# A second softmax in another layout: maxima from scores with tokens on partitions, spread and added by products

## The chip, the core and the metric

The kernel runs on one core of a Trainium2 chip. Its engines work side by side, each through its own list of instructions in order: TensorE (PE) multiplies matrices and writes to PSUM, VectorE (DVE) and ScalarE (ACT) read and write PSUM and SBUF, SyncE (SP) issues the transfers from and to HBM. The metric is the time of one execution on the device in microseconds (us).

## What is computed

Cut to what matters, the reference is:

```python
def sm_attn(qq, kk, vv):                      # 8 batches, 8 heads, 64 wide
    s = scale * np.matmul(qq, kk.transpose(0, 1, 3, 2))
    s = s - np.max(s, axis=-1, keepdims=True)
    a = np.exp(s)
    a = a / (np.sum(a, axis=-1, keepdims=True) + 1e-09)
    return np.matmul(a, vv)
p_packed = sm_attn(p, k, v)                   # 32 pack queries over 576 tokens
out = sm_attn(q, p_packed, p_packed)          # 576 queries over the 32 packed tokens
x = out, heads side by side                   # (4608, 512)
g = x @ w_gate; val = x @ w_val               # 512 -> 1536
result = (g * sigmoid(g) * val) @ w_out       # 1536 -> 512
```

The *second softmax* is the one inside the second call: for each query and head over 32 scores.

## The kernel before

The batches are worked on one after the other. The attention matrix `a` of the second call is never multiplied with `p_packed` on its own: `p_packed` is multiplied with the gate and value weights first (the words `M`, tiles `mh` and `ml`), and `a`, in the tile `a2f`, is then the moving operand of the matmuls `g` that give gate and value directly. `a2f` has the 32 packed tokens of 4 head pairs on its 128 partitions and 2 x 576 columns: for each parity of the head (`par`) the queries.

The weights lie in HBM as 64-bit floats. A chunk of 1 MB is loaded as pairs of 32-bit words and turned into float32 by five steps: two on ACT (lines 189 and 190), three on DVE (191 to 193). Until this is done for the first chunks the work on them can't begin, and each batch needs the results of the attention first. So the first batch has a prologue. Its order on all engines is written out by hand: first as code, then as a list of words, `PROGRAM`, each of which issues some instructions (`W2` is the next of the five steps of weight chunk 2, `V0` one of output weight chunk 0, `M:1.0` the products of the packed tokens with chunk 2, `Mh:1.0` ACT's copies of them out of PSUM, `g0` to `g23` the gate and value matmuls, `silu` and `h` what follows them on ACT and DVE, `out0` the first matmul with the output weights, `s1_...` the first softmax of the next batch, `load_...` transfers). A word's instructions go to their engines in this order.

The second softmax of the first batch, before: it is done in two halves of 288 queries. `s2_mm` multiplies queries and packed tokens, with the tokens on partitions (32 for each head pair). DVE transposes blocks of 32x32 (`s2_block`, line 498), so that the 32 scores of a query lie side by side in a row; takes their maximum and subtracts it (`s2_max`, lines 512 and 513); ACT takes the exponential (line 517); DVE adds, inverts and scales (`s2_sums`, `s2_scale`, lines 524 to 530) and transposes back (`back`, line 771) into `a2f`. ACT then makes a rounded copy (`two_high`, line 851).

PE has filler in the prologue: `warm_up(n)` multiplies the identity with itself n times (line 705), 18 times ahead of `g0` and 25 times behind it (`warm25`). A product of float32 operands is two records in the trace. The PSUM banks come from three pools: `acc` (4), `gv` (2) and `aux` (2).

Of the kernel before, what the change touches and what calls it, by code (L numbers as in the profile page):

```python
# [10 lines left out]
F32 = mybir.dt.float32  # L11
# [21 lines left out]
NA, NB = 256, 320  # L33
NT = B * S
# [6 lines left out]
    W2 g0 W1 two_max1 two_high0 W2 warm25 W1 two_exp1 W2 W2 silu0 V0 h0 W2 V0 W1 load_w3 load_v1 M:1.0 two_sums1  # L41
    Mh:1.0 M:0.1 V0 Mh:0.1 two_scale1 g1 V0 silu1 two_back1 s1_scores0 h1 g2 two_high1 s1_max0 W3 V0 load_w4
# [82 lines left out]
def tile_pack_attention_swiglu(ctx: ExitStack, tc: tile.TileContext, qT, kT, v, vq, pT, wgv, wout, out):  # L125
# [16 lines left out]
    nc.gpsimd.memset(minus_two, -2.0)  # L142

# [85 lines left out]
    def load_k(b):  # L229
# [3 lines left out]
        if b == 0:  # L233
            qs[b] = io_tile(0, [P, 2, NHP, HS], F32, "q_t")
# [465 lines left out]
    with tc.manual_schedule(engines={mybir.EngineType.PE}):  # L700
# [15 lines left out]
        with tc.manual_schedule(  # L716
# [313 lines left out]
```

## Time and profile before

| | us |
|---|---|
| timed runs: median (lowest to highest) of 3 | 744.02 (743.64 to 744.34) |
| profiled execution: span from the first to the last instruction | 742.9 |
| median less span | 1.1 |
| PE, DVE, ACT busy in the span | 732.6, 454.2, 372.2 |

The profile is of one execution on the same chip type, and its time is its span; what a timed run has beside it lies before the first and after the last instruction. A row of a timeline gives start, duration, engine, line of the kernel, operation, output and inputs, shapes and count; in brackets stands how long the engine was idle before it and what ended that. `PE` rows are matmuls, `PEld` rows weight loads. A duration includes the tail of an instruction, which the next one overlaps, so the distance of two starts is often the better price.

### The profile page before, as it was taken

The page shows a single profiled execution, that of the slowest core. Times are in us where ns is not written, and L with a number is a line of the kernel's source. Part 1 is how long each engine was busy: PE and PEld are TensorE (multiplying, and loading weights), DVE is VectorE, ACT ScalarE, POOL GpSimd, SP SyncE. Part 2 cuts the span into 40 slices and gives each one's busy share as a digit, 9 for nine tenths or more (in the row PEclk, how much of TensorE's full clock was granted, in tenths as well). Part 3 has the DMA queues.
Part 4 walks back from the last instruction along what each step waited for, and adds up shares of the span by engine and source line. Part 5 has one row for each costly group of instructions (what it writes and reads, how often), then busy time and mean ns, then how long its engine had stood idle before and what let it go on. Part 6 is the DMA issues. An engine that isn't in the chain of part 4 may idle for free.

```text
span 742.9 us, 14217 instructions
## 1 busy us (share of the span) xinstructions
PE 732.6 (99%) x5808; PEld 602.4 (81%) x5808; DVE 454.2 (61%) x1008; ACT 372.2 (50%) x666; POOL 2.0 (0%) x13
## 2 busy tenths in 40 slices
PE   7999999999999999999999999999999999999997
PEld 4855767888888888888888888888888888888886
DVE  4988879665755547663765637655574555644333
ACT  3777845744635446563462535653453534533331
POOL 0000000000000000000000000000000000000000
PEclk9999999999999999999999999999999999999999
DMA  9686582310112201301112021001001000010001
GB/s 348 256 306 248 196 326 73 119 52 21 65 57 84 72 1 65 124 4 71 66 43 97 3 71 64 34 29 71 1 2 69 6 1 1 1 57 2 0 1 72
DMA packets 20001, 59.10 MB, mean 80 GB/s; under 512 B 5984, under 2 KB 7008, under 8 KB 17376
## 3 DMA queue, kind: packets, MB, share of 16 engines
q1 hardware_dynamic: 19792, 58.12, 21.7%
q8 instruction: 46, 0.75, 0.4%
q14 instruction: 19, 0.16, 0.1%
q10 hardware_dynamic: 144, 0.07, 0.0%
HBM read 48.69 MB, written 9.49 MB: 78 GB/s over the span
## 4 chain that ended last, share of the span: by engine, by line
PE 96%; DVE 1%; ACT 0%; issue 0%; DVEq 0%
PE gv L617 36%; PE acc L636 33%; PE aux L259 7%; PE gv L802 6%; PE aux L636 5%; PE acc L843 4%; PE gv_aux L471 2%; PE gv_aux L259 1%; PE gv_aux L388 1%; PE acc L705 1%; PE warm_ps L705 1%; ACT mh L584 0%; PE aux L335 0%; DVE w L192 0%; DVE ml L558 0%
## 5 line engine op out<-in xcount | busy, mean ns | idle before, releaser
L624 ACT ACTIVATE sg<-gv 128x256 f32<-128x256 f32 (+1 forms) x168 | 69.3, 412 | 180.4 <-PE gv L617 168.2
L628 DVE TENSOR_TENSOR hf<-gv,sg 128x256 f32<-128x256 f32 x168 | 71.1, 423 | 130.0 <-PE gv L617 119.2
L617 PE MATMUL gv<-a2h,ml 128*128 128x256 f32 (+1 forms) x672 | 143.6, 295 | 1.2 <-DVE t L827 1.2
L617 PE MATMUL gv<-a2l,mh 128*128 128x256 f32 (+1 forms) x672 | 144.2, 296 | 0.0
L617 PE MATMUL gv<-a2h,mh 128*128 128x256 f32 (+1 forms) x672 | 144.1, 296 | 0.0
L636 PE MATMUL acc<-wo_h,hl 128*128 128x512 f32 x344 | 140.8, 409 | 0.0
L636 PE MATMUL acc<-wo_l,hh 128*128 128x512 f32 x344 | 135.7, 395 | 0.0
L636 PE MATMUL acc<-wo_h,hh 128*128 128x512 f32 x344 | 134.3, 390 | 0.0
L617 PEld LDWEIGHTS gv<-a2h,ml 128*128 128x128 f32 x672 | 117.0, 189 | 15.6 <-issue 1.4
L170 ACT CAST hh<-hf 128x256 fp32r<-128x256 f32 x168 | 67.7, 403 | 102.5 <-DVE hf L628 102.4
L617 PEld LDWEIGHTS gv<-a2h,mh 128*128 128x128 f32 x672 | 108.6, 190 | 0.0
L617 PEld LDWEIGHTS gv<-a2l,mh 128*128 128x128 f32 x672 | 108.3, 189 | 0.0
L598 DVE TENSOR_TENSOR hl<-hf,hh 128x256 fp32r<-128x256 f32 x168 | 70.1, 417 | 46.4 <-ACT hh L170 46.3
L636 PEld LDWEIGHTS acc<-wo_h,hl 128*128 128x128 f32 x344 | 64.7, 188 | 27.7 <-issue 18.6
L636 PEld LDWEIGHTS acc<-wo_h,hh 128*128 128x128 f32 x344 | 64.6, 188 | 15.0
L636 PEld LDWEIGHTS acc<-wo_l,hh 128*128 128x128 f32 x344 | 64.8, 188 | 7.9 <-issue 0.5
L558 DVE TENSOR_TENSOR ml<-aux,mh 128x512 fp32r<-128x512 f32 x92 | 59.0, 683 | 3.9 <-ACT mh L584 3.8
L259 PE MATMUL aux<-w,ppt 64*32 64x512 f32 (+1 forms) x784 | 52.4, 588 | 0.5 <-ACT mh L584 0.5
L584 ACT CAST mh<-aux 128x512 fp32r<-128x512 f32 x92 | 49.4, 589 | 6.5 <-PE aux L259 1.9
L624 ACT ACT_TABLE_LOAD x30 | 38.5, 1283 | 14.0 <-PE gv L617 10.1
L843 PE MATMUL acc<-wo_f,h 128*128 128x512 f32 x80 | 37.2, 595 | 0.0
L843 PEld LDWEIGHTS acc<-wo_f,h 128*128 128x128 f32 x80 | 14.3, 189 | 13.8 <-issue 13.2
(152 smaller groups left out, 769.3 us busy)
## 6 DMA issues: line engine op xcount, KB each, us to landing
st<-in_wgv SPq DMA_DIRECT2D x12, 1024.0 KB, 6.5
k_t<-in_kT SPq DMA_DIRECT2D x16, 576.0 KB, 4.9
q_t<-in_qT SPq DMA_DIRECT2D x16, 576.0 KB, 4.8
out<-ot SPq DMA_DIRECT2D x36, 256.0 KB, 2.1
v_t<-in_vq SPq DMA_DIRECT2D x6, 1280.0 KB, 5.9
st<-in_wout SPq DMA_DIRECT2D x6, 1024.0 KB, 5.4
v_t<-in_v SPq DMA_DIRECT2D x2, 1024.0 KB, 8.8
p_t<-in_pT SPq DMA_DIRECT2D x7, 64.0 KB, 1.9
```

Of the source, the lines that this page charges most:

```text
L170: e.copy(dst, src)
L259: nc.tensor.matmul(outs[par][32 * hp : 32 * hp + 32], lhs(r, hp), rhs(r, hp), start=True, stop=True)
L471: nc.tensor.matmul(p_p[D * par : D * par + D, NP * hp : NP * hp + NP], v_t[:, par, hp, k, :], a1[:, par, hp, k, :], start=(k == 0), stop=( ...
L558: pin(nc.vector.tensor_tensor(*lows.pop(0), op=ALU.subtract))
L584: nc.scalar.copy(m[0][at], src)
L598: low = lo.tensor_tensor(hl, src, hh.bitcast(F32), op=ALU.subtract)
L617: nc.tensor.matmul(pg[:, :n], m_[:, g, f, s * P : (s + 1) * P], a_[:, g, off : off + n], start=(i == 0), stop=(i == 5),)
L624: nc.scalar.activation(sg[:, :n], pgs[0][:, :n], AF.Silu)
L628: nc.vector.tensor_tensor(hf, pgs[1][:, o : o + 256], sg[:, o : o + 256], op=ALU.mult)
L636: nc.tensor.matmul(acc[:, :], h_[:, c : c + P], w_[fc // 2][:, fc % 2], start=(fc == 0 and i == 0), stop=(fc == NFC - 1 and i == 2),)
L802: nc.tensor.matmul(held[i][s][:, :n], m_[:, g, f, s * P : (s + 1) * P], a_[:, g, off : off + n], start=(j == 0), stop=(j == len(todo) - 1),)
L843: nc.tensor.matmul(accs[2 * is_b + c], half(i)[:, c * P : c * P + P], wos[fc // 2][:, fc % 2], start=(fc == 0), stop=(fc == NFC - 1),)
```

## The change

For the first 256 of the 576 queries of the first batch the second softmax is done in another layout; the other 320 keep the old steps, in one piece. The parts are `PART[0]` and `PART[1]`, the same split that the `g` matmuls use.

- `z_tok` computes the scores of the 256 queries a second time with queries on partitions (128 at a time), so that the 32 scores of a head lie in a row; `z_max` takes their negative maxima from PSUM.
- `z_mm(0)` computes the scores with tokens on partitions and leaves the PSUM sum open; `z_sub` adds to it the maxima, spread over the 32 tokens of each head by a product with the identity. `z_exp` is ACT's exponential out of PSUM into SBUF.
- `z_sum` adds the exponentials by a product with `head_of` (a 128x4 matrix of ones in each head's rows, made at the start by one DVE reduction); `z_inv` inverts; `z_bcast` spreads the inverses by products; `z_mul` multiplies into `a2f`. There is no transpose.
- The scale of the packed heads (`s1_scale`, DVE) becomes `one_scale`, two activations on ACT.
- Queries of the first batch lie in HBM in the order of the two parts and are loaded by two transfers of 512 and 640 KB.
- The prologue from there on is written in words. Both fillers behind the pack are gone. `M:0.1` stands ahead of `g1` and `M:1.0` behind it.

```diff
 PROGRAM = """
-    W2 g0 W1 two_max1 two_high0 W2 warm25 W1 two_exp1 W2 W2 silu0 V0 h0 W2 V0 W1 load_w3 load_v1 M:1.0 two_sums1
-    Mh:1.0 M:0.1 V0 Mh:0.1 two_scale1 g1 V0 silu1 two_back1 s1_scores0 h1 g2 two_high1 s1_max0 W3 V0 load_w4
+    W0 W0 W0 W0 one_scale W0 one_flip one_ppt z_tok z_mm two_mm1 z_max z_sub0 z_sub1 M:0.0 z_exp0 z_exp1 load_k1
+    load_wout0 two_block1 z_sum z_inv z_bcast Mh:0.0 two_max1 W1 z_mul accs g0 W1 two_high0 W2 W1 W2 W1 W2 W1 two_exp1
+    silu0 W2 two_sums1 M:0.1 h0 W2 V0 Mh:0.1 load_w3 load_v1 g1 M:1.0 two_scale1 V0 Mh:1.0 silu1 V0 two_back1
+    h1 V0 s1_scores0 g2 two_high1 s1_max0 W3 V0 load_w4
...
+    def z_tok():
+        q_t, ppt = z_q(0), ppts[0]
+        pss = zs["tok"] = [gv_ps(), gv_ps()]
+        for t in range(NA // P):
+            for hp in range(NHP):
+                for par in range(NPAR):
+                    r = slice(64 * par, 64 * par + 64)
+                    at = t * P + NP * hp
+                    nc.tensor.matmul(
+                        pss[par][:, at : at + NP], q_t[r, hp, t * P : (t + 1) * P], ppt[r, NP * hp : NP * hp + NP],
+                        start=True, stop=True,
+                    )
...
+    def z_spread(at, row, par, add):
+        for t in range(NA // P):
+            for hp in range(NHP):
+                x = t * NHP + hp
+                nc.tensor.matmul(
+                    at[NP * hp : NP * hp + NP, t * P : (t + 1) * P],
+                    zs["m"][:, row, par, x : x + 1].broadcast_to([P, NP]), ident,
+                    start=not add, stop=not add or t == NA // P - 1,
+                )
...
+    def z_exp(par):
+        nc.scalar.activation(st2[0][0][:, par, :NA], zs["mm", 0][par][:, :NA], AF.Exp, scale=SCALE)
+    def z_sum():
...
+                    x[:, at : at + NHP], st2[0][0][:, par, t * P : (t + 1) * P], head_of, start=True, stop=True,
...
-            s1_scale(0)
...
-            m_mm(0, 0, c0, True)
-            m_high(0, 0, c0)
-            s2_max(0, c0)
-            s2_exp(0, c0)
-            s2_mm(0, 1)
-            s2_block(0, 1)
-            load_k(1)
-            load_wout(0)
-            warm_up(18)
...
-            s2_sums(0, c0)
-            s2_scale(0, c0)
-            back(0)
+            def one_scale():
+                pp = pool.tile([P, NPAR, D], F32, tag="pp", bufs=1, name="pp")
+                for par in range(NPAR):
+                    nc.scalar.activation(
+                        pp[:, par], pps[0][0][:, par * D : (par + 1) * D], AF.Copy,
+                        scale=st1[0][2][:, 2, par : par + 1],
+                    )
+            def z_mul():
+                nc.vector.tensor_tensor(
+                    z_head["a2f"][:, :, PART[0]], st2[0][0][:, :, PART[0]],
+                    zs["inv"].rearrange("p (r n) -> p r n", r=NPAR), op=ALU.mult,
+                )
```

What stands in each engine's list now, at three places. First PE, from the last score products of the softmax to the first ones of the next batch (`s1_scores0`, the row with `k_t`). In the program before, `L705` is filler, `L802` are `g0` and `g1`, and `L259` with `w_82` and `w_81` are `M:1.0` and `M:0.1`:

```order
L705 MATMUL warm_ps<-ident 128x128 x18
L802 MATMUL gv<-a2f,mh 128x256 x4
L705 MATMUL acc<-ident 128x128 x25
L259 MATMUL aux<-w_82,ppt 32x256 x8
L259 MATMUL aux<-w_81,ppt 32x256 x8
L802 MATMUL gv<-a2f,mh 128x256 x4
L259 MATMUL aux<-k_t,p_t 32x288 x8
```

In the changed program the lines have moved (`L268` is the old 259, `L924` the old 802); `L569` is `z_tok`, `L588` are `z_sub` and `z_bcast`, `L606` is `z_sum`, and `w_83` and `w_84` are the old `w_81` and `w_82`:

```order
L569 MATMUL gv_aux<-ppt,q_t 128x32 x16
L268 MATMUL acc_aux<-q_t,ppt 32x256 x8
L268 MATMUL acc_aux<-q_t,ppt 32x320 x8
L588 MATMUL acc_aux<-ident,zm 32x128 x16
L268 MATMUL aux<-w_83,ppt 32x256 x8
L606 MATMUL acc_aux<-head_of,s_244 128x4 x4
L588 MATMUL acc_aux<-ident,zm 32x128 x16
L924 MATMUL gv<-a2f,mh 128x256 x4
L268 MATMUL aux<-w_83,ppt 32x256 x8
L924 MATMUL gv<-a2f,mh 128x256 x4
L268 MATMUL aux<-w_84,ppt 32x256 x8
L268 MATMUL aux<-k_t,p_t 32x288 x8
```

Both fillers are gone, three kinds of small products have come in, and the first `w_83` products behind `g0` are followed by `g1` and only then by those of `w_84`.

Second ACT, from the rounded copy of the first attention part (`a2h`) to the silu of `g1`. Before:

```order
L851 CAST a2h<-a2f 128x2x288
L190 ACTIVATE st<-st,minus_two 128x1024
L517 ACTIVATE s_229<-s_229 128x576
L818 ACT_TABLE_LOAD
L818 ACTIVATE sg<-gv 128x256
L189 ACTIVATE wo_f<-st 128x1024
L190 ACTIVATE st<-st,minus_two 128x1024
L584 COPY mh<-aux 128x256 x4
L818 ACTIVATE sg<-gv 128x256
```

After (`L973` is the old 851, `L194` and `L195` the old 189 and 190, `L638` the exponential of the 320 queries, `L940` silu, `L702` the copies out of PSUM):

```order
L973 CAST a2h<-a2f 128x2x256
L194 ACTIVATE w_84<-st 128x4x256
L195 ACTIVATE st<-st,minus_two 128x1024
L638 ACTIVATE s_244<-s_244 128x2x320
L940 ACT_TABLE_LOAD
L940 ACTIVATE sg<-gv 128x256
L194 ACTIVATE wo_f<-st 128x1024
L702 COPY mh<-aux 128x256 x2
L195 ACTIVATE st<-st,minus_two 128x1024
L702 COPY mh<-aux 128x256 x2
L940 ACTIVATE sg<-gv 128x256
```

The two conversion steps of `w_84` now both stand behind the copy of `a2f`, and the second pair of copies is divided from the first by a conversion step of the output weights.

Third DVE, where the first attention part is finished. Before, from the sums of the first half (line 524) on:

```order
L524 TENSOR_REDUCE r_230<-s_229 128x18
L525 TENSOR_SCALAR r_230<-r_230 128x18
L526 RECIPROCAL r_230<-r_230 128x18
L530 TENSOR_TENSOR s_229<-s_229,r_230 128x576
L771 STREAM_TRANSPOSE a2f<-s_229 128x288 x2
L191 TENSOR_SCALAR w_81<-w_81 128x4x256
L512 TENSOR_REDUCE r_230<-s_229 128x18
L513 TENSOR_TENSOR s_229<-s_229,r_230 128x576
L192 SCALAR_TENSOR_TENSOR w_81<-w_81,st 128x4x256
```

After, from the maxima (`L578`) on; `L629` transposes the 320 queries, `L612` and `L613` are `z_inv`, `L633` and `L634` maximum and subtraction of the 320 queries, `L884` is `z_mul`:

```order
L578 TENSOR_REDUCE zm<-gv_aux 128x8 x2
L629 STREAM_TRANSPOSE s_244<-acc_aux 128x320 x2
L612 TENSOR_SCALAR zm<-acc_aux 128x16
L613 RECIPROCAL zm<-zm 128x16
L633 TENSOR_REDUCE r_245<-s_244 128x20
L634 TENSOR_TENSOR s_244<-s_244,r_245 128x2x320
L884 TENSOR_TENSOR a2f<-s_244,acc_aux 128x2x256
L196 TENSOR_SCALAR w_83<-w_83 128x4x256
L197 SCALAR_TENSOR_TENSOR w_83<-w_83,st 128x4x256
```

Sum, scale and back transposes of the first part are gone from DVE's list; the maximum and subtraction of the second part now stand ahead of the end of the first.

## Rows read from the trace of the kernel before

**Rows 1.** The page: span, and busy time of the engines in it.

```profile
span 742.9 us, 14217 instructions
...
PE 732.6 (99%) x5808; PEld 602.4 (81%) x5808; DVE 454.2 (61%) x1008; ACT 372.2 (50%) x666; POOL 2.0 (0%) x13
```

**Rows 2.** Busy time by stretch: the stretch and its length in us, then for PE, PEld, DVE, ACT and POOL the busy us (and count of instructions), then the granted clock of TensorE as a share of full speed, the busy share of the DMA engines, and GB/s.

```profile
13.90:17.20 3.30, 1.66 (x45) 0.64 (x49) 2.89 (x5) 0.43 (x2) 0.00 (x0) 1.00 1.04 424
17.20:20.70 3.50, 3.50 (x28) 2.59 (x28) 3.35 (x7) 2.10 (x5) 0.00 (x0) 0.51 0.95 350
20.70:30.90 10.20, 10.20 (x88) 9.87 (x88) 9.97 (x15) 8.68 (x10) 0.00 (x0) 1.00 0.50 193
30.90:33.50 2.60, 1.58 (x34) 0.48 (x33) 2.53 (x6) 1.08 (x4) 0.00 (x0) 1.00 0.80 236
...
38.30:110.00 71.70, 71.70 (x472) 45.08 (x471) 60.16 (x93) 50.40 (x75) 0.00 (x0) 1.00 0.73 270
```

**Rows 3.** Timeline of PE in the prologue: start us, duration us, engine, line, operation.

```profile
12.19 1.73 PE L335 MATMUL gv_aux<-v_t,a 128*32 128x64 f32 x80 [0.60 <-DVE a L172]
15.07 0.33 PE L362 MATMUL acc_aux<-ident,pp 128*128 128x128 f32 x1 [1.15 <-DVE pp L352]
15.75 0.43 PE L259 MATMUL gv_aux<-q_t,ppt 64*32 64x288 f32 x1 [0.36 <-ACT ppt L366]
...
16.29 0.37 PE L259 MATMUL gv_aux<-w,ppt 64*32 64x256 f32 x1
...
18.18 5.45 PE L705 MATMUL warm_ps<-ident 128*128 128x128 f32 x36
23.47 1.89 PE L802 MATMUL gv<-a2f,mh 128*128 128x256 f32 x8
25.20 5.74 PE L705 MATMUL acc<-ident 128*128 128x128 f32 x50
30.87 0.66 PE L259 MATMUL aux<-w,ppt 64*32 64x256 f32 x16
32.05 0.93 PE L259 MATMUL aux<-w,ppt 64*32 64x256 f32 x16 [0.52 <-ACT mh L584]
33.49 1.99 PE L802 MATMUL gv<-a2f,mh 128*128 128x256 f32 x8 [0.50 <-ACT mh L584]
35.41 0.72 PE L259 MATMUL aux<-k_t,p_t 64*32 64x288 f32 x16
36.06 2.42 PE L802 MATMUL gv<-a2f,mh 128*128 128x320 f32 x8
38.31 1.90 PE L843 MATMUL acc<-wo_f,h 128*128 128x512 f32 x4
```

**Rows 4.** Timeline of DVE: the last transposes of the first half, maximum and subtraction of the second with a conversion step behind them, the maxima of the next batch's scores, and the last step of the first output weights.

```profile
21.89 0.84 DVE L771 STREAM_TRANSPOSE a2f<-s 128x288 f32<-128x288 f32 x2
...
23.22 0.74 DVE L512 TENSOR_REDUCE r<-s 128x18 f32<-128x576 f32 x1
24.00 0.76 DVE L513 TENSOR_TENSOR s<-s,r 128x576 f32<-128x576 f32 x1
24.67 1.22 DVE L192 SCALAR_TENSOR_TENSOR w<-w,st 128x1024 int32<-128x1024 int32 x1
...
36.22 0.82 DVE L282 TENSOR_REDUCE mx<-aux 128x1 f32<-128x288 f32 x2 [0.20 <-PE aux L259]
36.96 1.22 DVE L193 SCALAR_TENSOR_TENSOR wo_f<-st,wo_f 128x1024 int32<-128x1024 int32 x1
```

**Rows 5.** Timeline of ACT from the copy of the packed heads (`ppt`) to the copies of `M:0.1`.

```profile
15.43 0.27 ACT L366 COPY ppt<-acc_aux 128x128 f32<-128x128 f32 x1 [2.40 <-PE acc_aux L362]
...
20.68 1.23 ACT L190 ACTIVATE st<-st,minus_two 128x1024 f32<-128x1024 uint32 x1
21.82 1.17 ACT L189 ACTIVATE w<-st 128x1024 f32<-128x1024 f32 x1
22.88 0.67 ACT L851 CAST a2h<-a2f 128x576 fp32r<-128x576 f32 x1
23.44 1.25 ACT L190 ACTIVATE st<-st,minus_two 128x1024 f32<-128x1024 uint32 x1
24.79 0.69 ACT L517 ACTIVATE s<-s 128x576 f32<-128x576 f32 x1
25.50 1.28 ACT L818 ACT_TABLE_LOAD   x1
26.79 0.38 ACT L818 ACTIVATE sg<-gv 128x256 f32<-128x256 f32 x1
27.68 1.18 ACT L189 ACTIVATE wo_f<-st 128x1024 f32<-128x1024 f32 x1 [0.51 <-DMA st<-in_wout]
...
33.06 0.65 ACT L584 COPY mh<-aux 128x256 f32<-128x256 f32 x2 [0.79 <-PE aux L259]
```

**Rows 6.** Queries of the first batch: issue on SP's queue (both transfers in one row), and the time from issue to landing of the two.

```profile
3.46 1.05 SPq L252 DMA_DIRECT2D q_t<-in_qT  x2
...
DMA to landing us min/median/max: 10.3/10.7/11.1
```

**Rows 7.** Groups of instructions by line and shape over the whole span: count, then busy us, mean ns of one, idle before.

```profile
L558 DVE TENSOR_TENSOR ml<-aux,mh 128x512 fp32r<-128x512 f32 x92 | 59.0, 683 | 3.9 <-ACT mh L584 3.8
...
L471 PE MATMUL gv_aux<-a,v_t 128*64 128x32 f32 x480 | 15.1, 223 | 0.0
```

More of the change, by code (lines that the diff above doesn't have):

```diff
@@ L248, in load_q, with by_head @@
     def load_q(b):
-        if b:
-            qs[b] = io_tile(1, [P, 2, NHP, HS], F32, "q_t")
+        if not b:
+            for c in range(2):
+                at = slice(NHP * PART[c].start, NHP * PART[c].stop)
+                nc.sync.dma_start(qs[b][:, at], q0[:, at])
+            return
+        qs[b] = io_tile(1, [P, 2, NHP, HS], F32, "q_t")
         for c in range(2):
-            nc.sync.dma_start(qs[b][:, c], qT[b, :, c])
-    def by_head(outs, lhs, rhs):
+            nc.sync.dma_start(qs[b][:, c], qT[b - 1, :, c])
+    def by_head(outs, lhs, rhs, stop=True):
         for hp in range(NHP):
@@ new lines, in z_sub @@
+    def z_sub(par):
+        z_spread(zs["mm", 0][par], 0, par, True)
+    def z_exp(par):
+        nc.scalar.activation(st2[0][0][:, par, :NA], zs["mm", 0][par][:, :NA], AF.Exp, scale=SCALE)
+    def z_sum():
+        x = zs["sum"] = z_bank()
+        for par in range(NPAR):
+            for t in range(NA // P):
+                at = (par * 2 + t) * NHP
+                nc.tensor.matmul(
+                    x[:, at : at + NHP], st2[0][0][:, par, t * P : (t + 1) * P], head_of, start=True, stop=True,
+                )
@@ new lines, in z_inv, with z_bcast, z_view @@
+    def z_inv():
+        m, n = zs["m"], NPAR * NA // P * NHP
+        nc.vector.tensor_scalar(m[:, 1].rearrange("p r x -> p (r x)"), zs["sum"][:, :n], 1e-9, None, op0=ALU.add)
+        nc.vector.reciprocal(m[:, 2], m[:, 1])
+    def z_bcast():
+        x = zs["inv"] = z_bank()
+        for par in range(NPAR):
+            z_spread(x[:, par * NA : (par + 1) * NA], 2, par, False)
+    def z_view(c):
+        s2, r2 = st2[0]
+        x = s2[:, :, PART[c]].rearrange("p r (k n) -> p r k n", n=NP)
+        k = x.shape[2]
+        return x, [r2[:, i, : NPAR * k].rearrange("p (r k) -> p r k", r=NPAR) for i in range(3)], [P, NPAR, k, NP]
@@ new lines, in z_block, with z_top, z_exp1, z_sums1 @@
+    def z_block():
+        for par in range(NPAR):
+            nc.vector.transpose(st2[0][0][:, par, PART[1]], zs["mm", 1][par][:, :NB])
+    def z_top():
+        x, (m, _, _), shape = z_view(1)
+        nc.vector.tensor_reduce(m, x, axis=AX.X, op=ALU.max)
+        nc.vector.tensor_tensor(x, x, m.unsqueeze(3).broadcast_to(shape), op=ALU.subtract)
+    def z_exp1():
+        x = st2[0][0][:, :, PART[1]]
+        nc.scalar.activation(x, x, AF.Exp, scale=SCALE)
+    def z_sums1():
+        x, (m, s, r), _ = z_view(1)
+        nc.vector.tensor_reduce(s, x, axis=AX.X, op=ALU.add)
+        nc.vector.tensor_scalar(m, s, 1e-9, None, op0=ALU.add)
+        nc.vector.reciprocal(r, m)
```

86 lines of the change are left out of this document (59 added, 27 removed).

## Prediction

> **What bounds the kernel now.** I read the page first, then the busy table by stretch, then the timelines of the engines up to 40 us, and the chain that ended last. TensorE (PE) is busy for 732.6 of 742.9 us, and from 38.3 to 110 us it has no idle time at all [rows 1, 2]. So after the prologue the time is a sum of matmuls, and the change can only move the moment at which that unbroken run begins. I take as its beginning the first output matmul (`out0`, the row of line 843 at 38.31 us [rows 3]): from there on the words of the program are the same before and after. VectorE (DVE) finishes the first output weights (line 193, 36.96 + 1.22 = 38.18 us [rows 4]) just ahead of it, so DVE sets this moment. Before it PE's busy time is partly filler: 36 records of identity products at 18.18 us and 50 at 25.20 us [rows 3].
>
> The profiled execution spans 742.9 us and the timed runs have a median of 744.02 us; the difference of 1.1 us lies outside the span and stays. I add the shift of `out0` to 744.02.
>
> **The change part by part, first with the clock at full speed.**
>
> *Ahead of the second softmax.* The scale of the packed heads goes from DVE to ScalarE (ACT). Before, it had to wait for DVE's conversion and the flip began at 15.07, though the products it needs had ended at 12.19 + 1.73 = 13.92 us [rows 3]. ACT is idle there until 15.43 [rows 5]. Two scaled copies of 128x64 aren't in the trace; they lie between 0.27 (one copy of 128x128, the row of `ppt`) and 0.54 (two of them); I take 0.40, as they overlap. Flip 0.33 [rows 3], `ppt` 0.27 [rows 5], and three hand-overs of about 0.04 each: the first product starts at 15.05 instead of 15.75. The first half of the queries had landed at 3.46 + 10.3 = 13.8 us and the second at about 15.2 [rows 6]; the new first transfer is smaller, so it isn't late.
>
> *New: scores with tokens on partitions (`z_tok`).* 16 matmuls, 32 records, each loads 64x128 weights and moves 32 columns. The nearest row loads 128x64 and moves 32 columns: 480 records in 15.1 us, 31 ns each [rows 7]. For twice the columns that is 63 ns, 2.0 us in all, if the two halves of the rows load one after the other, and 1.0 us if side by side. I take 1.5. The far bound is the full 128x128 product, (30.87 - 25.20) / 50 = 0.113 us per record [rows 3], 3.6 us.
>
> *The chain to the first attention part.* With `z_tok` from 15.05 to 16.55 (+0.2 of tail), DVE's two maxima end at 17.6 (two reductions of 288 columns take 0.82 [rows 4]); beside them PE does the two score products for 256 and 320 queries, 0.54 us by the row of 288 columns (15.75 to 16.29 [rows 3]), together 1.1: 17.65. The two `z_sub` spread the maxima: 16 records each of 128 moving columns on four column strips. The pack does 80 records of 64 columns in 1.73 us [rows 3], 22 ns each; twice the columns is at most 43 ns, and I take 28: 0.45 each. 18.6. The second exponential ends at 19.25 (0.5, below ACT's 0.69 for 576 columns [rows 5]). Sums by products (`z_sum`) 0.8, half of it behind that exponential: 20.05. `z_inv` 0.5. Then DVE does maximum and subtraction of the other 320 queries, 0.74 + 0.76 for 576 columns [rows 4], so 1.65 for 640, and hides `z_bcast` (32 records, about 1.0) under them. The multiply from PSUM, 0.68 [rows 7], ends at about 22.8 us. Before, the first half's last transpose ended at 21.89 + 0.84 = 22.73 [rows 4]. So the new softmax is not earlier; what it spares is DVE's work after it.
>
> *From there to `g1`.* ACT's queue decides: cast 0.5, two conversion steps 1.06 + 1.14, exponential 0.78 for 640 columns, table load 1.28, silu 0.38, one step of the output weights 1.06, and only then the copy `Mh:0.1` 0.65 [rows 5]: 6.75 us, 29.5. Beside it DVE finishes `W1` with four conversion steps of at most 1.22 each [rows 4], by 27.7, and PE has `M:0.1` done by 28.4, ahead of ACT's turn for its copy at 28.9. `g1` starts at 29.55 instead of 33.49. But `M:1.0`, which stood ahead of `g1`, now stands behind it, and the chain goes on through it: `g1` 1.83, `M:1.0` 0.65, `Mh:1.0` 0.65, `silu1` 0.4, `h1` 0.4, DVE's second step of the output weights (1.22 less 0.08 of overlap), the maxima 0.74, its third step 1.22 [rows 3, 4, 5]. With hand-overs that is 36.6 us. PE's own path (`s1_scores0` 0.65, `g2` 2.25 [rows 3]) ends at 35.8, inside it. At full clock `out0` comes 1.7 us earlier.
>
> *Removed: both fillers.* As work they cost nothing, being off DVE's path. But the granted clock hangs on what PE did. Between 13.9 and 17.2 us PE was busy for 1.66 of 3.30 us, and from 17.2 to 20.7 its clock was 0.51 of full speed, the 1.2 GHz level; under the fillers it came back to 1.00 [rows 2]. From 30.9 to 33.5, with 1.58 of 2.60 busy, it did not fall [rows 2]. After the change PE does `g0` (22.85 to 24.7), `M:0.1` (0.66 [rows 3]) and nothing else until 29.55: 0.66 busy in 4.9 us, far less than in the stretch after which it fell. The filler of 50 records covered just this gap. The Trainium skill, TensorE: Matmul & The Clock Gate, section "Why this matters for your kernels", says the same of idle gaps between bursts of matmuls: they bring the engine back to half rate. By that rule the fall is certain; the trace agrees in one stretch and shows no gap as empty as this one.
>
> If the clock falls in that gap, `g1` and `M:1.0` run at half speed, 1.83 + 0.5 us longer, and both stand in the chain. `out0` is then at 36.6 + 2.3 = 38.9, 0.6 later than before. While they run, PE is busy throughout, as it was from 17.2 to 20.7 before the clock rose, so I let it be back for `g2`.
>
> *Queues.* `load_k1` waits for the query buffer, which the second score product frees at 17.65 (+0.1): before, it was issued at about 18.3 behind the same product at half clock. The output weights behind it landed at 27.68 [rows 5]; ACT asks for them at about 27.9, so this cover is nearly used up: a load later by 1 us would cost 0.8.
>
> **The rivals.**
>
> 1. *Full clock after all.* The gain of 1.7 stands whole: 742.3. For it: the 1.58 of 2.60 us without a fall [rows 2]. Against it: the gap of 4.9 us is emptier. It decides from the point where no low stretch touches `g1`; if the fall comes only inside `g1`, about half the gain is left (743.3).
>
> 2. *The clock also falls at 17.2, inside the softmax's own products.* It did so before [rows 2], and `z_tok` moves few columns. Score products, `z_sub`, `M:0.0` and `z_sum` are then up to 1.7 us longer and lie in the chain to the multiply; most of it adds to the loss: 744.6 + 1.6 = 746.2. Against it: PE now has products from 15.05 without a break.
>
> 3. *`z_tok` is bound by its weight loads.* At 0.113 us a record it is 2.1 us longer, all of it in the chain: 744.4 at full clock and 746.7 with the low one. The skill's page on TensorE, section "LDWEIGHTS (loading the stationary operand)", counts one column per cycle of 1.2 GHz whatever the rows: an estimate of 107 ns for 128 columns, 3.4 us for 32 loads. By that page rival 3 holds; the 31 ns per load of 64 columns [rows 7] is below its 53 ns, so the trace here speaks against it.
>
> 4. *Nothing moves*: if DVE's third step of the output weights waits on something unchanged, such as their transfer at 27.68 with a later issue, gain and loss cancel within 0.2%. It is part of the forecast's chance.
>
> **How the numbers follow.** The likeliest is the low clock in the gap and only there: 744.6 us, chance 0.42 (with the cases near it, 742.6 to 745.5). Full clock in `g1`, or a shorter `z_tok` with a short low stretch: 0.28. Low clock in the softmax too: 0.20. Slow loads in `z_tok`: 0.10. A change of 0.2%, 1.5 us, is about what a measurement of this kernel can tell from none: faster means under 742.5, slower over 745.5. So faster 0.28, same 0.42, slower 0.30. The range reaches from 742.0 (full clock, `z_tok` at 1.2 us) to 746.6 (rival 2 with some of rival 3).
>
> **What the changed profile would show.** Right: the first `z_tok` record at about 15.05; the 32 of them in 1.0 to 2.0 us; the multiply into `a2f` ending at 22 to 23.5 us at full clock; ACT without a gap from there to `Mh:0.1`; a granted clock near 0.5 in a stretch that covers `g1`; `out0` at 38 to 39.5. Wrong: a clock of 1.00 throughout 24 to 36 us, with `out0` near 36.6 (rival 1); a low clock before 20 us and a multiply after 24 (rival 2); `z_tok` over 2.5 us (rival 3); or PE idle after `out0`, where I assume none.

## The result, and the profile after

| | before | after |
|---|---|---|
| timed runs, median (lowest to highest), us | 744.12 (743.64 to 744.34), 4 runs | 749.43 (747.89 to 749.96), 4 runs |
| ratio to before, 95% interval | | 1.0065 (1.0047 to 1.0082) |
| profiled execution, span, us | 742.9 | 747.6 (its own time: 749.36) |
| first output matmul, `out0`, us | 38.31 [rows 3] | 41.99 |
| busy PE, DVE, ACT, us | 732.6, 454.2, 372.2 [rows 1] | 733.4, 451.7, 372.1 |

The change made the kernel 5.3 us slower, outside the predicted range of 742.0 to 746.6. The page of the changed kernel, span and busy time, as in [rows 1]:

```profile
span 747.6 us, 14251 instructions
...
PE 733.4 (98%) x5826; PEld 600.4 (80%) x5826; DVE 451.7 (60%) x1003; ACT 372.1 (50%) x669; POOL 2.0 (0%) x13
```

DVE is spared 2.5 us, PE does no less than before. Busy time by stretch, columns as in [rows 2] (the granted clock is the third number from the right):

```profile
13.90:17.20 3.30, 2.26 (x27) 2.07 (x29) 1.94 (x2) 0.78 (x3) 0.00 (x0) 0.85 1.05 430
17.20:20.70 3.50, 3.50 (x52) 1.97 (x56) 1.21 (x4) 0.00 (x0) 0.00 (x0) 0.50 0.69 273
20.70:26.70 6.00, 4.43 (x84) 2.85 (x73) 2.99 (x8) 3.58 (x6) 0.00 (x0) 0.78 0.86 292
26.70:30.30 3.60, 3.46 (x8) 2.52 (x8) 3.51 (x5) 3.56 (x5) 0.00 (x0) 0.56 0.33 135
30.30:33.50 3.20, 0.99 (x18) 0.53 (x18) 3.13 (x7) 3.19 (x6) 0.00 (x0) 0.97 0.61 195
33.50:37.20 3.70, 3.70 (x24) 2.32 (x23) 2.80 (x5) 1.04 (x1) 0.00 (x0) 0.57 0.99 415
37.20:42.00 4.80, 3.61 (x40) 1.76 (x25) 3.48 (x6) 4.33 (x8) 0.00 (x0) 1.00 0.06 18
```

By the shares, the clock is at the 1.2 GHz level in three places, where before had one [rows 2]: from about 16.2 to 23.1 us over most of the new softmax, from 26.5 to 29.9 over `g0`, from 33.3 to 36.7 over `g1`. The timeline of PE, answering to [rows 3]; `L569` is `z_tok`, `L588` `z_sub` and then `z_bcast`, `L606` `z_sum`, `L924` the `g`, `L965` `out0`:

```profile
14.58 0.33 PE L371 MATMUL aux<-ident,pp 128*128 128x128 f32 x1 [0.69 <-ACT pp L873]
15.27 2.79 PE L569 MATMUL gv_aux<-ppt,q_t 64*128 64x32 f32 x32 [0.35 <-ACT ppt L375]
17.98 2.17 PE L268 MATMUL acc_aux<-q_t,ppt 64*32 64x256 f32 x32
20.08 1.93 PE L588 MATMUL acc_aux<-ident,zm 128*32 128x128 f32 x32
21.94 1.11 PE L268 MATMUL aux<-w,ppt 64*32 64x256 f32 x16
22.98 1.07 PE L606 MATMUL acc_aux<-head_of,s 128*128 128x4 f32 x8
24.70 1.08 PE L588 MATMUL acc_aux<-ident,zm 128*32 128x128 f32 x32 [0.65 <-DVE zm L613]
26.84 3.47 PE L924 MATMUL gv<-a2f,mh 128*128 128x256 f32 x8 [1.05 <-DVE a2f L884]
30.50 0.67 PE L268 MATMUL aux<-w,ppt 64*32 64x256 f32 x16 [0.19 <-DVE w L198]
33.19 3.68 PE L924 MATMUL gv<-a2f,mh 128*128 128x256 f32 x8 [2.02 <-ACT mh L702]
36.80 0.66 PE L268 MATMUL aux<-w,ppt 64*32 64x256 f32 x16
...
41.99 1.55 PE L965 MATMUL acc<-wo_f,h 128*128 128x512 f32 x3 [0.68 <-DVE wo_f L198]
```

`g0` and `g1` take 3.5 and 3.7 us for what took 1.9 and 2.0. The end of the new softmax on DVE, and the two pairs of PSUM copies on ACT (`Mh:0.1`, `Mh:1.0`):

```profile
26.01 0.68 DVE L884 TENSOR_TENSOR a2f<-s,acc_aux 128x512 f32<-128x512 f32 x1
...
32.76 0.64 ACT L702 COPY mh<-aux 128x256 f32<-128x256 f32 x2
...
37.55 0.65 ACT L702 COPY mh<-aux 128x256 f32<-128x256 f32 x2 [3.01 <-PE aux L268]
```

So three lengths describe the prologue: start of `z_tok` at 15.27; from there to the end of the multiply 11.42 us (26.69); from there to `out0` 15.30 us. The second one is the surprise: the prediction's sum had 7.75.

`out0` is 3.68 us late, the span 4.7. Behind `out0` the rows on PE show no new wait, and yet the kernel falls back further. The silu of the same chunk near the two ends of the run, in before and after (ACT; start in the first column):

```profile
68.66 0.44 ACT L818 ACTIVATE sg<-gv 128x320 f32<-128x320 f32 x1
725.87 0.44 ACT L624 ACTIVATE sg<-gv 128x320 f32<-128x320 f32 x1 [1.39 <-PE gv L617]
```

```profile
72.43 0.44 ACT L940 ACTIVATE sg<-gv 128x320 f32<-128x320 f32 x1
730.50 0.44 ACT L742 ACTIVATE sg<-gv 128x320 f32<-128x320 f32 x1 [1.41 <-PE gv L735]
```

657.21 us between them before, 658.07 after: 0.86 us more, at a granted clock of 1.00 throughout. This "fall back over the steady part" is the second thing to explain.

### The profile page after: what moved, and what is told of

It is laid out like the page before. It is cut to its first block, busy times and chain, and to the rows that moved or that the text cites. A ratio compares the mean times of both kernels' runs of the same rounds, so it can differ in the third digit from the quotient of the medians.

```text
span 747.6 us, 14251 instructions
## 1 busy us (share of the span) xinstructions
PE 733.4 (98%) x5826; PEld 600.4 (80%) x5826; DVE 451.7 (60%) x1003; ACT 372.1 (50%) x669; POOL 2.0 (0%) x13
## 4 chain that ended last, share of the span: by engine, by line
PE 94%; DVE 1%; ACT 1%; issue 0%; DVEq 0%
PE gv L735 36%; PE acc L754 33%; PE aux L268 7%; PE gv L924 5%; PE aux L754 4%; PE acc L965 4%; PE gv_aux L480 2%; PE gv_aux L397 1%; PE gv_aux L268 1%; ACT mh L702 0%; PE aux L344 0%; ACT L940 0%; DVE wo_f L197 0%; DVE wo_f L198 0%; DVE ml L676 0%
## 5 line engine op out<-in xcount | busy, mean ns | idle before, releaser
L268 PE MATMUL aux<-w,ppt 64*32 64x512 f32 (+1 forms) x800 | 53.2, 589 | 0.2 <-DVE w L198 0.2
L702 ACT CAST mh<-aux 128x512 fp32r<-128x512 f32 x92 | 49.4, 589 | 6.8 <-PE aux L268 2.2
L965 PE MATMUL acc<-wo_f,h 128*128 128x512 f32 x80 | 37.2, 596 | 0.7 <-DVE wo_f L198 0.7
L965 PEld LDWEIGHTS acc<-wo_f,h 128*128 128x128 f32 x80 | 14.3, 189 | 14.7 <-issue 13.2
```

Of the source, the lines that this page charges most:

```text
L702: nc.scalar.copy(m[0][at], src)
L965: nc.tensor.matmul(accs[2 * is_b + c], half(i)[:, c * P : c * P + P], wos[fc // 2][:, fc % 2], start=(fc == 0), stop=(fc == NFC - 1),)
```

## Experiments on the clock

The theory: the low stretches make most of the loss. The rival: the chain of waits is longer by itself. Ratios are to before, run beside the kernel in the same session. Fillers (identity products, two records each) were put back or taken away.

**Before without its fillers.**

```diff
-    W2 g0 W1 two_max1 two_high0 W2 warm25 W1 two_exp1 ...
+    W2 g0 W1 two_max1 two_high0 W2 W1 two_exp1 ...
-            warm_up(18)
```

> The kernel before without its two fillers (18 and 25 identity products). Theory 1, the granted clock is what costs: PE is idle in the old gap between g0 and the next products too, the clock falls there and g1 or the products ahead of it run at half speed; 1.5 to 2.5 us slower than before, about 746.0, with a low stretch that begins between 24 and 31 us. Theory 2, the fillers are dead weight and the changed kernel is slow by the length of its own chain: within 0.5 us of before, 744.1.

Measured: 746.77 us, ratio 1.0027 (1.0009 to 1.0045); `out0` at 39.40. PE's `g0` and `g1`, and two stretches with columns as in [rows 2]:

```profile
22.11 3.75 PE L801 MATMUL gv<-a2f,mh 128*128 128x256 f32 x8 [4.70 <-DVE a2f L770]
32.43 3.78 PE L801 MATMUL gv<-a2f,mh 128*128 128x256 f32 x8 [0.50 <-ACT mh L584]
```

```profile
18.00:22.00 4.00, 0.00 (x0) 0.00 (x0) 3.81 (x9) 3.12 (x4) 0.00 (x0) 0.73 1.01 400
30.00:38.00 8.00, 6.99 (x49) 3.83 (x44) 5.30 (x12) 3.26 (x7) 0.00 (x0) 0.57 0.71 279
```

The clock fell earlier than expected, at 19.9 us, in the idle time ahead of `g0`, and was back only at 36.9. The fillers' removal alone costs 2.8 us by the medians (744.01 for before beside it) and 2.0 by the ratio: some two fifths to a half of the change's loss needs nothing of the new softmax.

**The changed kernel with fillers in the gaps between `g0` and `g1`** (6 products behind `g0`, 8 behind `M:0.1`), **with fillers ahead of `g0` only** (3 ahead of the flip, 1 ahead of `z_tok`, 3 ahead of `z_bcast` and of `g0`), **and with both.**

```diff
-  accs g0 W1 ...  M:0.1 h0
+  accs g0 warm6 W1 ...  M:0.1 warm8 h0
```

```diff
-  W0 one_flip one_ppt z_tok ... z_inv z_bcast ... z_mul accs g0
+  W0 pre3 one_flip pre1 one_ppt z_tok ... z_inv fill3 z_bcast ... z_mul fill3 accs g0
```

> The changed kernel with fillers in the gap between g0 and g1 only: 6 identity products behind g0, 8 behind M:0.1. Theory 1: the stretch of low clock that covered g1 (3.68 us in the changed kernel, 1.9 at full clock) goes, and g1 ends 1.7 to 1.8 us earlier: about 747.6. Theory 2: g1 is not in the chain, 749.4 as the changed kernel. The low stretch in the softmax's own products stays in both.

> The changed kernel with fillers in the softmax stage only: 3 identity products ahead of the flip, 1 ahead of z_tok, 3 ahead of z_bcast, 3 ahead of g0. Theory 1: if this keeps the clock up, z_tok, the score products, z_sub, M:0.0 and z_sum take about 3 us less and the multiply ends near 23.5 instead of 26.7: about 746.4; if the clock falls all the same during z_tok, little changes (749 to 750), which leaves open whether the clock or the loads make z_tok long. Theory 2: 749.4 or up to 1 us more.

> The changed kernel with both sets of fillers (all of the two kernels beside it). Theory 1: no low stretch from 15 to 40 us; the multiply ends near 23.5 and out0 comes at 37 to 38 us, so 743.5 to 744.5, the gain that was worked out for full clock less what z_tok takes beyond 1.5 us. Theory 2: 749.4 or more, as PE has more to do.

Measured:

| | median (us) | ratio, 95% | `z_tok` starts | to the end of the multiply | from there to `out0` | `out0` |
|---|---|---|---|---|---|---|
| after | 749.43 | 1.0065 (1.0047 to 1.0082) | 15.27 | 11.42 | 15.30 | 41.99 |
| fillers in the gaps | 746.25 | 1.0046 (1.0022 to 1.0071) | 15.15 | 9.95 | 13.69 | 38.79 |
| fillers ahead of `g0` | 748.28 | 1.0052 (1.0035 to 1.0069) | 15.30 | 9.70 | 16.62 | 41.62 |
| both | 746.03 | 1.0036 (1.0020 to 1.0053) | 14.86 | 9.50 | 13.85 | 38.21 |

The fillers ahead of `g0` hold the clock through the softmax in this execution, and it then falls in the gap, for longer than in the changed kernel itself. By stretch, in that run:

```profile
14.00:22.80 8.80, 8.02 (x134) 5.92 (x135) 3.76 (x9) 2.89 (x8) 0.00 (x0) 1.00 0.83 312
22.80:28.00 5.20, 4.17 (x49) 3.14 (x48) 5.07 (x8) 4.47 (x6) 0.00 (x0) 1.00 0.87 311
28.00:31.00 3.00, 0.67 (x16) 0.18 (x16) 2.93 (x6) 2.97 (x4) 0.00 (x0) 0.88 0.47 107
31.00:36.00 5.00, 4.50 (x24) 2.75 (x24) 3.60 (x7) 1.89 (x4) 0.00 (x0) 0.50 0.96 395
36.00:40.00 4.00, 3.48 (x27) 1.58 (x20) 2.63 (x5) 2.60 (x5) 0.00 (x0) 0.50 0.00 0
```

After the emptiest stretch (0.67 of 3.00 us busy) the clock stays at 0.50 from 31 to 40 us, though PE is busy for 7.98 of the 9. So these fillers alone moved the loss: 748.28, where 746.4 was expected. With the fillers in the gaps alone:

```profile
17.00:20.70 3.70, 3.70 (x68) 2.10 (x66) 1.67 (x4) 0.38 (x1) 0.00 (x0) 0.54 0.86 286
20.70:25.00 4.30, 2.85 (x64) 1.99 (x56) 2.43 (x5) 3.21 (x5) 0.00 (x0) 1.00 0.95 303
25.00:40.00 15.00, 13.09 (x103) 9.06 (x104) 14.23 (x24) 12.68 (x19) 0.00 (x0) 1.00 0.60 213
```

The clock is 1.00 from 20.7 us on, and these fillers bring nearly all of the gain by themselves (746.25; 747.6 was expected). Not all of that is theirs. Up to `g0` this kernel has the instructions of the changed one, and yet the clock was down for 3.4 us in its softmax (17.3 to 20.7) where it was down for 6.8 in the changed kernel (16.2 to 23.1), and the multiply ended 1.5 us sooner after the start of `z_tok`. How long the clock stays down in the softmax thus differs between executions of the same instructions. With both sets, the clock is 1.00 from 14 to 38 us, and its multiply and PE's way to `out0` read:

```profile
14.86 1.98 PE L569 MATMUL gv_aux<-ppt,q_t 64*128 64x32 f32 x32
16.76 1.19 PE L268 MATMUL acc_aux<-q_t,ppt 64*32 64x256 f32 x30
18.41 0.72 PE L268 MATMUL acc_aux<-q_t,ppt 64*32 64x320 f32 x2 [0.45 <-issue]
19.06 1.08 PE L588 MATMUL acc_aux<-ident,zm 128*32 128x128 f32 x32
...
23.68 0.68 DVE L884 TENSOR_TENSOR a2f<-s,acc_aux 128x512 f32<-128x512 f32 x1
...
31.09 1.99 PE L924 MATMUL gv<-a2f,mh 128*128 128x256 f32 x8 [0.37 <-ACT mh L702]
...
38.21 1.98 PE L965 MATMUL acc<-wo_f,h 128*128 128x512 f32 x4 [0.68 <-DVE wo_f L198]
```

By the medians the clock is worth 3.4 of the 5.3 us (749.43 less 746.03); the ratios, 1.0065 and 1.0036, make it 2.2, with intervals that overlap. The rival holds the rest: 743.5 to 744.5 was expected with both sets, and the changed kernel is still 2.0 us behind before (746.03 against 744.01). In two of the ten timed runs of this kernel the time was 749.8 and 750.9 with a mean clock of 0.993 and 0.991, so the fillers don't hold it in every execution.

**What is before at full clock?** Its own profiled execution has a low stretch [rows 2], in which 36 filler records took 5.45 us [rows 3]. The control is before with 3 products ahead of the flip and 1 ahead of the score products; beside it, before with only the scale on ACT.

```diff
+            warm_up(3)
             s1_flip(0)
+            warm_up(1)
             s1_ppt(0)
```

> The control for the run with all fillers: the kernel before with the same three products ahead of the flip and one ahead of the score products. In the profiled execution of before the granted clock was 0.50 from 17.4 to 20.6 us, and its 36 filler records took 5.45 us; in the one with the scale on ACT it was 1.00 there and they took 4.29. If such stretches come and go with PE's pauses around the flip, this kernel has none: out0 near 37.2 to 37.6, spans of 741.6 to 742.0 with little spread, a median near 743.6. The difference to the changed kernel with all fillers (746.03) is then the cost of the change at full clock, some 2.4 us. If before has no such loss in most executions, the median stays at 744.1.

```diff
-            s1_scale(0)
+            pp = pool.tile([P, NPAR, D], F32, tag="pp", bufs=1, name="pp")
+            for par in range(NPAR):
+                nc.scalar.activation(
+                    pp[:, par], pps[0][0][:, par * D : (par + 1) * D], AF.Copy, scale=st1[0][2][:, 2, par : par + 1],
+                )
+            pps[0].append(pp)
```

> The kernel before with one part of the change alone: the scale of the pooled values by two ACT activations instead of one DVE operation, so that the flip no longer waits behind two of DVE's conversions. Flip and first score products start about 0.6 us earlier (15.1 instead of 15.75), g0 near 22.9 instead of 23.47. From g0 on the path runs over the conversions of w and wo on ACT and DVE, which this doesn't touch, so out0 is expected within 0.4 us of 38.31 and the median within 0.4 of the kernel before. If instead the 0.6 us reach out0, the median is near 743.4. If the clock theory is at work here too (products end earlier, a gap ahead of the fillers), a low stretch would show and the median would rise by 1 us or more.

Measured: 744.45 us (1.0003, 0.9994 to 1.0013) and 743.94 us (1.0001, 0.9990 to 1.0011). In the control the fillers and `out0` read:

```profile
17.42 4.29 PE L705 MATMUL warm_ps<-ident 128*128 128x128 f32 x36
...
37.10 1.90 PE L845 MATMUL acc<-wo_f,h 128*128 128x512 f32 x4
```

At full clock before's `out0` is at 37.10 (37.16 with the scale on ACT), not at 38.31: its recorded execution carried 1.2 us of low clock. The medians did not fall with it. Executions of before with a mean clock of 1.000 were among its timed runs anyway, but the control's ten runs, at 0.997 to 1.000, have spans from 741.7 to 743.7 us, and why their median isn't below that of before (744.04) stays open. The earlier flip, alone, is worth nothing that can be measured. Against the control the change at full clock has `out0` 1.1 us later. Its span is 2.3 us longer in the profiled executions (744.0 against 741.7), each the fastest of its ten; by the medians, from two sessions, it is 1.6 (746.03 against 744.45).

## Experiments on the steady part

All kernels with the change fall back by 0.74 to 1.05 us between the two silus of the rows above, whatever their fillers; before without fillers falls back by 0.07, the control by 0.03, before with the scale on ACT by 0.29 (taken from the next silu of 320, as the first came some 0.8 us late in that run). The words there are those of before. What differs is where tiles lie: the order of PSUM banks, and addresses in SBUF.

**Addresses shifted; order of the `gv` and `aux` banks; order of the `acc` banks in before; the old order of the `acc` banks in the changed kernel with all fillers.**

```diff
+    spare = const.tile([P, 4], F32, name="spare")
+    nc.vector.memset(spare, 0.0)
...
-                pool.tile([P, 3, NPAR], F32, tag="rs1", bufs=3, name="rs1"),
+                pool.tile([P, 64], F32, tag="rs1", bufs=3, name="rs1")[:, :6].rearrange("p (i r) -> p i r", i=3),
```

> The kernel before with two tiles padded so that every later tile in SBUF stands at the address that it has in the changed kernel (704 bytes further for the tiles of the steady part); the work is the same. In all four kernels with the change, the time behind out0 is 705.6 to 705.8 us in the profile, against 704.6 to 704.7 in the kernel before and in the one without its fillers. If the addresses cause this, this kernel shows 705.6 behind out0 and a median near 745.0; if they don't, 704.6 and 744.0. out0 is expected at 38.3 either way.

```diff
-            warm_up(18)
+            warm_up(16)
+            warm_up(1, gv_ps())
+            warm_up(1, ps_aux.tile([P, 512], F32, tag="aux", name="aux"))
```

> The kernel before with two of its 18 products ahead of g0 written to one more gv tile and one more aux tile, so that from there on the two gv banks and the two aux banks of PSUM alternate in the changed kernel's order; the work and the count of products are the same. If the order of the banks causes the 1.0 us behind out0 that the four kernels with the change share, this kernel shows 705.6 behind out0 and a median near 745.0; if not, 704.6 and 744.0. The order of the four acc banks, which also differs in the changed kernel, stays that of before, so a miss here leaves that order open.

```diff
-    "warm": lambda n: warm_up(n, accs[3]),
+    "warm": lambda n: [warm_up(m, accs[i]) for i, m in ((0, 8), (2, 8), (3, n - 16))],
```

> The kernel before with the 25 products behind g0 spread over three of the four acc banks (8, 8 and 9), so that the four accumulators take the banks in the order 3, 2, 0, 1 from there on, as in the kernels with the change, instead of 3, 2, 1, 0. Work and counts are the same. If this order is behind the 0.75 to 1.05 us by which every kernel with the change falls back between 69 and 726 us, this kernel falls back by 0.7 or more over the same stretch and its median is near 744.8; if not, by 0.0 to 0.3 as the other kernels without the change, and the median stays near 744.1.

```diff
-  g0 warm6 W1
+  g0 warm_a3 warm_b3 W1      # on accs[0] and accs[2]
```

> The reverse: the changed kernel with all fillers (746.03, out0 at 38.21), its six products behind g0 written to two other acc banks (3 and 3), so that the accumulators take the banks in the order 3, 2, 1, 0, that of the kernel before. If the order of banks makes the loss over the steady part, 0.3 us or less of it is left and the median is near 745.2; if not, it stays at 1.0 and the median at 746.0.

| | falls back by (us) | median (us) | ratio, 95% |
|---|---|---|---|
| before, addresses + 704 bytes | 0.22 (from the next silu, as above) | 744.72 | 1.0010 (1.0000 to 1.0020) |
| before, other `gv` and `aux` order | 0.09 | 744.50 | 1.0002 (0.9993 to 1.0012) |
| before, other `acc` order | 0.03 | 744.02 | 0.9999 (0.9989 to 1.0009) |
| changed with fillers, old `acc` order | 1.01 | 746.00 | 1.0030 (1.0018 to 1.0042) |

The banks are excluded, by runs from both sides for `acc`, by one in before for `gv` and `aux`. The shift shows no loss of its own: its 0.22 is no more than the 0.29 of before with the scale on ACT, whose tiles lie where they did. But the shift is not the whole difference: the change also creates the tiles of `t4` and of the `h0` and `wo` pairs ahead of those of `mh`, so they stand in another order.

**The whole layout of the changed kernel in before, and the layout of before in a kernel with the change** (the reordered one of the next section). The first has the two padded tiles from above, without the memset, and these lines; the same creations further down are taken out. The second moves them behind the tiles of `mh`.

```diff
...
+            t4_of(0)
+            h0 = [pair(F32, "h0") for _ in range(NFC // 2 - 1)]
+            for k in (*range(NFC // 2 - 2), NFC // 2 - 1, NFC // 2 - 2):
+                wos[k] = pair(F32, "wo_f")
             for _ in range(4):
                 step("W", 0)
```

> The kernel before with the whole SBUF layout of the changed kernel: the 704 bytes, and the tiles of t4 and of the h0 and wo pairs created ahead of pp, r2 and mh (mh at 171,552 instead of 111,456, the first pair at 116,320 instead of 125,792). Not one instruction differs in what it does. If the layout makes the loss over the steady part, this kernel falls back by 0.7 to 1.0 us between 69 and 726 us against the profile of before, and its median is near 745.0. If not, it falls back by 0.3 or less and stays at 744.1.

> The reordered kernel (742.79) with the SBUF layout of before: the pairs, t4 and a2 created behind the tiles of mh again, the maxima's tile in the place of pp. All tiles of the steady part then stand 32 bytes from where they stand in before. If the layout makes the loss, 0.2 us or less of its 0.87 are left and the median is near 742.1; if not, 0.87 stays and the median is 742.8.

Measured: before with that layout 745.30 us, ratio 1.0015 (1.0005 to 1.0025); the reordered kernel goes from 742.79 to 742.22. The two silus in the former, and in the latter:

```profile
68.33 0.44 ACT L819 ACTIVATE sg<-gv 128x320 f32<-128x320 f32 x1
726.37 0.44 ACT L625 ACTIVATE sg<-gv 128x320 f32<-128x320 f32 x1 [1.41 <-PE gv L618]
```

```profile
65.60 0.44 ACT L942 ACTIVATE sg<-gv 128x320 f32<-128x320 f32 x1
722.85 0.44 ACT L742 ACTIVATE sg<-gv 128x320 f32<-128x320 f32 x1 [1.39 <-PE gv L735]
```

658.04 us in before with the new layout, 657.25 in the changed kernel with the old: the loss went over with the layout, in both directions. The layout of SBUF makes it: 0.8 us in each, where kernels of one layout differ by up to 0.3. It is spread thin. Over all rows of PE between 60 and 735 us, the starts of the first and second pair of products of a 320 group (`a2h,ml` and `a2l,mh`) lie 292.1 ns apart in before, 295.7 in before with the new layout, 295.6 after, and 292.5 in the changed kernel with the old layout (168 of each); from the second to the third it is 292.7, 291.4, 291.2 and 292.2, which gives a third of it back. Between the two silus the `g` products make some 0.5 us of the loss and the output products some 0.3. Which of the moved tiles does it was not told apart.

## Experiments on the chain at full clock, and a faster order

**The score products of the 320 queries behind `z_sub`.**

```diff
-  z_tok z_mm two_mm1 z_max z_sub0 z_sub1 M:0.0
+  z_tok z_mm z_max z_sub0 z_sub1 two_mm1 M:0.0
```

> The changed kernel with all fillers (746.03), with one word moved: the score products of the 320 queries (two_mm1) behind z_sub instead of ahead of it, so that z_sub waits only for its own 256 queries and the maxima. In the run with all fillers the score products lay between 16.76 and 19.06 us and the maxima ended at 17.62. If the score products in front of z_sub are the mis-sized term, z_sub starts near 17.8 instead of 19.06; z_sum then stands behind two_mm1 and M:0.0 on PE and starts near 20.0 instead of 20.66; the multiply ends 0.6 to 0.7 us earlier than 24.36, and the chain behind it keeps its 13.85 us: out0 near 37.6, median near 745.4. If the time hangs on something else in the row (the 0.45 us wait that the profile puts down to issue goes along with whatever stands there), z_sub starts after 18.5 and out0 stays at 38.2.

Measured: 745.47 us, ratio 1.0017 (1.0008 to 1.0027), `out0` at 37.97. PE:

```profile
17.07 0.66 PE L268 MATMUL acc_aux<-q_t,ppt 64*32 64x256 f32 x16
17.66 0.64 PE L588 MATMUL acc_aux<-ident,zm 128*32 128x128 f32 x14
18.70 0.84 PE L588 MATMUL acc_aux<-ident,zm 128*32 128x128 f32 x18 [0.40 <-issue]
```

`z_sub` starts at 17.66, as expected, and the median falls by the expected 0.6. That agreement is luck: `out0` comes only 0.24 us earlier, at 37.97 and not 37.6, and the two medians are from two sessions. The multiply ends 9.13 us after `z_tok` starts, against 9.50: the wait put down to issue now stands inside `z_sub`. In both kernels it stands behind exactly 62 records from the start of `z_tok` (32 + 30, and 32 + 16 + 14), some 3.1 us after that start. So it doesn't belong to the products that stand there. Whether it hangs on the place in PE's list or on that time, and on what, no row shows.

**Another order of the words.** With the clock at full speed DVE sat idle for 4.4 us between 15.6 and 21.8 and then worked to `out0` with one gap of 0.77 us (behind `silu1`).

```diff
-  one_ppt z_tok z_mm two_mm1 z_max z_sub0 z_sub1 M:0.0 z_exp0 z_exp1 load_k1 load_wout0 two_block1 z_sum z_inv ...
+  one_ppt W1 z_tok z_mm two_mm1 load_wout0 z_max z_sub0 z_sub1 M:0.0 z_exp0 z_exp1 load_k1
+  two_block1 two_max1 z_sum Mh:0.0 two_exp1 W1 W1 z_inv fill3 z_bcast two_sums1 z_mul fill3 accs g0 warm2 W2 W2 W1 W1
+  silu0 M:0.1 warm3 two_scale1 h0 Mh:0.1 g1 warm4 W2 V0 W2 silu1 W2 M:1.0 two_back1 V0 Mh:1.0 load_w3 load_v1
+  h1 s1_scores0 g2 warm3 two_high0 two_high1 V0 V0 V0 s1_max0 W3 load_w4
```

> The changed kernel with fillers (as in the run with all of them, out0 at 38.21 there) and its words in another order: the first ACT step of W1 ahead of the exponentials, load_wout0 ahead of load_k1, the other part's maxima, exponential and sums ahead of z_inv and z_mul, W1's DVE steps right behind z_mul, Mh:0.1 and silu1 ahead of the wo steps of ACT. DVE sat idle for 4.4 us between 15.6 and 21.8 in that run; this order fills about 2.5 of them. If DVE's row of conversions sets out0 at full clock, out0 comes near 35.5 and the median is near 743.3 (746.0 less 2.7), or 742.3 if the 1.0 us behind out0 goes too. If out0 is set by something else (the landing of wo, the matrix products' own row), it stays within 1 us of 38.2 and the median near 746.

Measured: 743.86 us, ratio 1.0002 (0.9987 to 1.0016), `out0` at 36.42: DVE's row did set it, but 0.65 us of the gain went into the three fillers behind `g2`, which ended at 36.4 when the output weights had been ready at 35.55. Then with `g2` ahead of the next scores, without these fillers, and with the two products behind `g0` written to two other `acc` banks:

```diff
-    h1 s1_scores0 g2 warm3 two_high0 ...
+    h1 g2 s1_scores0 two_high0 ...
```

> The reordered kernel (743.86, out0 at 36.42) with the accumulators' banks in the order of before, and with g2 ahead of the next batch's score products and without the three fillers behind g2. V0's last step ended at 35.55 there, and out0 stood behind g2 and the fillers: out0 is expected near 35.6. With the loss over the steady part gone as well the median is near 742.4; if the banks are not its cause, 743.1; if g2 ahead of the scores gains nothing, 743.2 or 743.9.

Measured: 742.79 us, ratio 0.9986 (0.9976 to 0.9995), `out0` at 35.40; it fell back by 0.87 over the steady part all the same. With the layout of before (the run above) 742.22 us, ratio 0.9976 (0.9966 to 0.9986): 1.9 us faster than before, 7.2 faster than after.

```profile
14.76 1.98 PE L569 MATMUL gv_aux<-ppt,q_t 64*128 64x32 f32 x32
...
24.37 1.97 PE L926 MATMUL gv<-a2f,mh 128*128 128x256 f32 x8
...
35.16 1.98 PE L967 MATMUL acc<-wo_f,h 128*128 128x512 f32 x4 [0.54 <-DVE wo_f L198]
```

So the idea of the change can pay, with fillers, order and layout put right. Whether the old softmax would gain as much from a new order wasn't run.

## Why the prediction was wrong

Its likeliest case put `out0` at 15.05 + 7.75 + 16.1 = 38.9; measured 15.27 + 11.42 + 15.30 = 41.99.

- **Start of `z_tok`.** 15.27 for 15.05. The two scaled copies took 0.52, not 0.40. Right.
- **The step that failed: "the low clock in the gap and only there".** The clock fell in the softmax too, as rival 2 said, and its price was right for this execution: 11.42 us against 9.70 with the clock held, 1.7. (With the fillers in the gaps alone, where the stretch was half as long, it was 9.95 against 9.70.) The argument against it, that PE has products from 15.05 without a break, was no protection. The clock came down at about 16.2 us, behind two short pauses around the flip (0.69 and 0.35 us), while `z_tok` kept PE busy, and stayed down for some 6.8 us of unbroken products. The case got 0.20 and should have been the likeliest: before's own fall at 17.2 [rows 2] stood behind the same flip.
- **Mis-sized: the chain to the multiply at full clock.** 9.50 us for 7.75. From the start of `z_tok` to the end of the score products it took 4.20 (14.86 to 19.06) for 2.6: `z_tok` 1.90 for 1.5, the score products 2.30 for 1.1, of which the stall behind the 62nd record is 0.45 and the two records behind it 0.65. The rest, from `z_sub` on, was 5.30 for 5.15.
- **`z_tok` is not bound by loads at 0.113 us (rival 3).** 32 records took 1.90 us at 2.4 GHz, 59 ns each, near the 63 worked out from [rows 7]. In the profiled execution of the run with the old `acc` order the clock was 0.50 under all of `z_tok`, and there they took 3.56 us, 111 ns each. The Trainium skill, TensorE: Matmul & The Clock Gate, section "LDWEIGHTS (loading the stationary operand)", puts the time of a load in ns at its columns over 1.2, an estimate of 107 ns for 128 columns: the trace agrees at the lower level only, and the measurement decides at the upper.
- **From the multiply to `g1`.** ACT's queue was to take 6.75 us (its terms add up to 6.85): 6.50 after, 6.73 with all fillers. Right. From `g1` to `out0` at full clock 7.05: measured 7.12. Right.
- **The low clock in the gap.** +2.3 predicted; 15.30 against 13.85 with all fillers is 1.45 in the changed kernel, where the clock had come back by 37, and 2.8 in the run with the softmax held, where it stayed low through `g2`. "I let it be back for `g2`" holds in one and not in the other.
- **Behind `out0`** the prediction took the words as the same and so the time as the same. The words were; the tiles' places in SBUF weren't: 0.86 us.
- **The base.** 744.02 less 742.9 was read as time outside the span. Every run listed with its span has some 1.8 us outside it, so the profiled execution took 744.7, longer than each of the three timed runs, with a low stretch of its own. Adding the shift to the median lost 0.7 us.
- **Queues.** No stall on `load_k1` or the output weights appeared: ACT's step on them at 31.75 waited for nothing.

Of the 4.8 us between 744.6 and 749.43, these terms make 3.1 (`out0`), 0.86 and 0.7; 0.2 is left. The range was too narrow at its top by the prediction's own sums: 746.6 lies below rival 3 with the low clock (746.7).

## What to carry to other kernels

A filler taken out of a prologue is part of the change: price the stretch it covered at both levels of the clock, and give the low one the larger chance wherever the row before shows it falling at the same place. One profiled execution gives one length of such a stretch: a second one of the same instructions can give half of it. Count the profiled execution's own low stretches before subtracting from it. And where a change creates tiles in another order, compare the addresses: a steady part with the same instructions isn't yet a steady part of the same speed.

## Not expected of the hardware

- The place of tiles in SBUF changed the pace of an unbroken run of matmuls by 0.13% (0.83 us over 657) with not one instruction changed in kind or order.
- The clock stayed at 1.2 GHz for 9 us with PE busy for 7.98 of them (31 to 40 us, fillers ahead of `g0` only), and was down for 3.4 us in before (17.2 to 20.6), some 2.4 of them under identity fillers. With all fillers and the old `acc` order it was down for 13.7 us in the profiled execution (11.5 to 25.2), most of them with PE busy.
- PE paused for 0.40 to 0.65 us behind the 62nd record from the start of `z_tok` in the kernels with the change that held the clock through the softmax, whichever instruction stood there.
